# Gated linear attention and a four-expert MLP on one core: D parts of the second layers last, attention steps of neighbouring blocks paired, state update in half-width matmuls

## Chip, cores, metric

One core of one Trainium2 chip. The metric is device time in microseconds (us) of the whole program, lower is better; medians of several executions, and ratios with a 95% interval.

## The reference

```python
# attention: B, H, S, D = 4, 8, 768, 48
for t in range(S):
    state = alpha[:, :, t, :, None] * state + einsum('bhd,bhe->bhde', k[:, :, t], v[:, :, t])
    y[:, :, t] = einsum('bhd,bhde->bhe', q[:, :, t], state)
x = y.transpose(0, 2, 1, 3).reshape(3072, 384)
# experts: 4 of them, 384 -> 1024 -> 384
p = probs / (probs.sum(-1, keepdims=True) + 1e-9)
for e in range(4):
    out += p[:, e:e+1] * (maximum(x @ w1[e], 0) @ w2[e])
```

## The kernel before

The 24 blocks of 128 rows ("units", six chunks of time for each of four batches) go through attention in order. They form seven groups, gi = 0 to 6, of 2, 4, 4, 4, 4, 4 and 2 blocks. While TensorE does the first and second layers of a group's four experts, the 17 steps of the next group's attention are strewn between its matmuls by a schedule that counts an estimated clock. From gi = 2 on both layers run on split fp32 values: an operand is kept as a top part, a low part, and a "D" part; a product is one sum over the top and low parts and a second sum with D.

The second layer of an expert, before: two blocks at a time, their main sums, then their D sums, in four PSUM banks (the memory that matmuls write their sums to) shared with the first layer. Half of each D part is made at once in the first layer, the rest during the second.

```python
kinds = [((0, 1), range(FCH - 2)), ((0, 1), range(FCH - 2, FCH)), ((2,), range(FCH))]
steps = [(part, i, fc) for parts, tiles in (kinds if halves_ else [((3,), range(FCH))])
         for part in parts for i in range(len(slots)) for fc in tiles]
for n, (part, i, fc) in enumerate(steps):
    ...
    if later and n % 4 == 3:
        make_dif(*later.popleft())                      # the D parts
    ...
    nc.tensor.matmul(sums[i][part // 2], lhsT=h[:, part], rhs=w, start=..., stop=...)
    if part >= 1 and fc == FCH - 1:
        # VectorE: acc += p * sum, frees the bank
        add_up(gi, e, slots[i], part // 2, sums[i][part // 2 if halves_ else 0])
```

The attention steps that matter here, by their number j: 7 first scores (sc, 64 instructions), 10 last copy of the queries by ScalarE (qb), 11 last scores (far and sc), 15 result (yps), 16 state update (sps). Tiles: dec0 to dec6 (products of decays), xT (the split input of the first layer), hT (hidden parts). The tiles of the pool that holds the stage's operands are laid out one after the other in SBUF: ..., dec0 to dec6 (products of decays; dec6 is 16 bytes a partition), xT (the split input of the first layer, its moving operand), x_raw, then the pool of hT (hidden parts) and acc.

Of the kernel before, what the change touches and what calls it, by code (L numbers as in the profile page):

```python
# [10 lines left out]
F32 = mybir.dt.float32  # L11
# [9 lines left out]
def kernel(  # L21
# [37 lines left out]
    nc = tc.nc  # L59

    B, H, S, D = q.shape
    E, DM, F = moe_w1.shape
    P = 128
    NCB = S // P
    NP = H // 2
# [78 lines left out]
    accs = {}  # L144


    BEATS = [*(0.055 * (j + 1) for j in range(11)), 0.69, 0.75, 0.8, 0.87, 0.94, 1.0]
    MARGIN = 6.0
    waiting = deque()
    clock = 0.0  # L150
# [1 line left out]


    split1 = lambda gi, e: gi > 0
    split2 = lambda gi, e: gi > 1
    makes = [lambda gi, e: gi == 0, lambda gi, e: gi == 1]


# [110 lines left out]
    def attention(u):  # L269
# [41 lines left out]
        def next_q(li):  # L311
            m = LEVELS[li]
            qv = halves(QT, m)[:, :, :, 1, :]
            dv = halved(decs[li])
            nc.vector.tensor_mul(qv, qv, spread(dv[:, :, :, 0], m))  # L315
            dec = work.tile([P, NP, P // (2 * m)], F32, name=f"dec{li}", bufs=1)
            nc.vector.tensor_mul(dec, dv[:, :, :, 0], dv[:, :, :, 1])
            decs.append(dec)

# [138 lines left out]

        if cb < NCB - 1:
            KB = AT  # L460
            sps = ps.tile([P, NP, 2, D], F32, name="sps", tag="w")
            for p in range(NP):
                nc.tensor.matmul(sps[:, p], lhsT=KB[:, p, :], rhs=rv[:, 2 * p:2 * p + 2, :D],  # L463
                                 start=True, stop=True)
            for i in range(2):
                rows = slice(HD * i, HD * (i + 1))
                old, add = st[rows, :, i, :], sps[rows, :, i, :]
                if cb == 0:
                    nc.vector.tensor_copy(out=old, in_=add)
                else:  # L470
                    nc.vector.tensor_mul(old, old, decs[-1][rows].broadcast_to([HD, NP, D]))
                    nc.vector.tensor_add(old, old, add)
# [30 lines left out]
    def up(gi, e, fc, slots=None):  # L503
# [26 lines left out]
        if not split1(gi, e):  # L530
            for kc in range(KC):
                nc.tensor.matmul(one, lhsT=w[:, kc], rhs=xraws[gi][:, kc, lo:hi],  # L532
                                 start=(kc == 0), stop=(kc == KC - 1))
            nc.scalar.activation(out=whole, in_=one, func=ACT.Relu)
        else:
            two = ps.tile([P, NT], F32, name="two", tag="g", bufs=4)[:, :n]
            for out, terms in ((one, (1, 0)), (two, (2,))):
                for part in terms:
                    for kc in range(KC):
                        nc.tensor.matmul(out, lhsT=w[:, part, kc], rhs=x_part(gi, part, kc),  # L540
                                         start=(part == terms[0] and kc == 0),
                                         stop=(part == terms[-1] and kc == KC - 1))

            ends_first = gi < LAST
            for steps in finish:
                for _ in steps if ends_first else [next(steps)]:
                    pass
            ahead = [] if ends_first else list(finish)
            finish.clear()
            t = work.tile([P, NT], F32, name="t")[:, :n]  # L550
            nc.scalar.activation(out=t, in_=one, func=ACT.Copy, scale=FINE)  # L551
            if split2(gi, e):
                nc.vector.tensor_add(t, t, two)  # L553
                for steps in ahead:
                    next(steps, None)
                finish.append(hidden_parts(t, parts))
            else:
                nc.vector.tensor_add(whole, t, two)  # L558
                finish.append(rectified(whole))
# [16 lines left out]
    def hidden_parts(x, parts):  # L576
        top, low, dif = parts
        nc.scalar.activation(out=top, in_=x, func=ACT.Relu, scale=TRIM)  # L578
        yield
        nc.vector.scalar_tensor_tensor(out=low, in0=x, scalar=0.0, in1=top.bitcast(F32),  # L580
                                       op0=ALU.max, op1=ALU.subtract)

        n = x.shape[-1]
        at = n // 2 if n == NT else 0
        if at:
            make_dif(*(part[:, :at] for part in parts))
        later.append([part[:, at:] for part in parts])

    def make_dif(top, low, dif):
        nc.vector.scalar_tensor_tensor(out=dif, in0=top.bitcast(F32), scalar=1 / 4096.0,  # L590
# [6 lines left out]
    def down(gi, e, slots, between):  # L597


        first = first_piece(gi, e)  # L600
        halves_ = split2(gi, e)
        if slots[0] == 0 and makes[1](gi, e):
            making.extend(split_piece(1, first + k) for k in range(NQ))
        if slots[0] == 0 and makes[0](gi, e) and 0 < e < E - 1:
            making.extend(split_piece(0, first + k) for k in range(2, NQ))
        sums = [[ps.tile([P, DM], F32, name=f"ops{j}", tag="g", bufs=4)
                 for j in range(2 if halves_ else 1)] for _ in slots]

        kinds = [((0, 1), range(FCH - 2)), ((0, 1), range(FCH - 2, FCH)), ((2,), range(FCH))]
        steps = [(part, i, fc) for parts, tiles in (kinds if halves_ else [((3,), range(FCH))])  # L610
                 for part in parts for i in range(len(slots)) for fc in tiles]
        for n, (part, i, fc) in enumerate(steps):
            c, f = divmod(fc, FPQ)
            h = hidden[c][:, :, f, slots[i] * P:(slots[i] + 1) * P]
            advance(cost(1, gi, e) / FCH / (3 if halves_ else 1))
            while between and n >= between[0][0] * len(steps):
                between.popleft()[1]()
            if n == len(steps) // 2:
                background()
            if later and n % 4 == 3:  # L620
                make_dif(*later.popleft())
            if halves_:
                w = wt[1][first + c].rearrange("p t (c d) -> p t c d", d=DM)[:, part, f]
                nc.tensor.matmul(sums[i][part // 2], lhsT=h[:, part], rhs=w,  # L624
                                 start=(fc == 0 and part != 1), stop=(fc == FCH - 1 and part != 0))
            else:
                w = wt[1][first + c].rearrange("p (c d) -> p c d", d=DM)[:, f]
                nc.tensor.matmul(sums[i][0], lhsT=h[:, 2].bitcast(F32), rhs=w,  # L628
                                 start=(fc == 0), stop=(fc == FCH - 1))
            if part >= 1 and fc == FCH - 1:  # L630
                add_up(gi, e, slots[i], part // 2, sums[i][part // 2 if halves_ else 0])
        while between:
            between.popleft()[1]()
        background()
        if slots[-1] == len(groups[gi]) - 1 and gi != LAST - 1:
            while makes[1](gi, e) and (making or splitting):
                background()

            for c in range(NQ):
                del wt[1][first + c]  # L640
                if c < NQ // 2 or gi == LAST:
                    load_piece(1, first + NQ + c)
                else:
                    late.append(first + NQ + c)
# [31 lines left out]
    def deal():  # L676
# [3 lines left out]
        wanted = [0.0]  # L680
        ends = [0.0, 0.0]
        events = []
        t = 0.0
        for (gi, e), after in zip(tasks, tasks[1:]):
            part = 1 - 1 / len(groups[0]) if gi == e == 0 else 1
# [5 lines left out]
        for gis in [*([gi] for gi in range(1, LAST - 1)), [LAST - 1, LAST]]:  # L691
            gi, due = gis[0], wanted[gis[-1]] - MARGIN
            n = sum(len(groups[i]) for i in gis)
            first = wanted[gi - 1] if gi > 1 else 0.0
            space = (due - first) / (n if gi > 1 else (n + 1) / 2)
            if gi == 1:
                space /= 2
            for k in range(n):
                u = sum(map(len, groups[:gi])) + k
                end = due - (n - 1 - k) * space  # L700
                begin = max(end - 2 * space, ends[-2])
                ends.append(end)
                run = attention(u)
                events += [(begin + (end - begin) * beat, u, run) for beat in BEATS]
        return sorted(events, key=lambda x: x[:2])

    def advance(spent):
# [5 lines left out]
    with tc.manual_schedule():  # L713
# [48 lines left out]
        for (gi, e), after in zip(tasks, [*tasks[1:], (None, None)]):  # L762
            rest = gi == e == 0
            for fc in range(FCH):
                up(gi, e, fc, slice(1, len(groups[0])) if rest else None)
                advance(cost(0, gi, e) / (2 if rest else 1))
            each = 2 if split2(gi, e) else 1
            turns = [range(k, k + each) for k in range(rest, len(groups[gi]), each)]
            for k, slots in enumerate(turns):

                between = deque()
                if after[1] == 0:
                    for step, at in enumerate((0.0, 0.52, 0.62, 0.72)):
                        at = at * len(turns) - k
                        if 0 <= at < 1:
                            between.append((at, lambda step=step: split_x(after[0], step)))
# [31 lines left out]
```

## Time and profile before

| | before |
|---|---|
| time, median (lowest to highest) | 1073.79 us (1073.01 to 1075.13), 3 runs |
| span of the profiled run | 1071.6 us |
| busy: TensorE, weight loads, VectorE, ScalarE | 98%, 84%, 72%, 53% |
| DMA | 235 GB/s mean |

Busy time adds up the durations of instructions; TensorE's matmuls overlap (the 512-column ones last 400 ns in the profile, and the next starts 229 ns after), so its busy share says that it is never idle for long, not how fast it runs. For that, take the distance from start to start in the timeline. The lines on which the argument rests are in the prediction below.

### The profile page before, as it was taken

What the parts mean: (1) busy time and instruction counts of PE and PEld (TensorE: products, weight loads), DVE (VectorE), ACT (ScalarE), POOL (GpSimd) and SP (SyncE); (2) the same over time, 40 slices, a digit from 0 to 9 for tenths busy, and PEclk for the clock granted to TensorE, in tenths of its full rate; (3) what the DMA queues carried; (4) which work ended last, traced back from release to release, by engine and by line L of the source; (5) the groups of instructions that cost most, each with busy time, mean ns of one, the idle gap of its engine ahead of it and who ended that gap; (6) DMA issues with size and microseconds to landing.
All of it is one profiled execution on the core that took longest, in us unless ns stands there. A gap on an engine that the chain in (4) does not pass through costs nothing.

```text
span 1071.6 us, 21614 instructions
## 1 busy us (share of the span) xinstructions
PE 1048.1 (98%) x8460; PEld 899.1 (84%) x8460; DVE 775.2 (72%) x1711; ACT 566.7 (53%) x1202; POOL 32.7 (3%) x71
## 2 busy tenths in 40 slices
PE   8899999999999999999999999999999999999998
PEld 8777777676776798898898898898889889898988
DVE  5488776656566978778877777986787866666565
ACT  5687866575656554536546445555464543323232
POOL 2010000000000100000000000000000000000000
PEclk9999999999999999999999999999999999999999
DMA  8597699687696967758759558586594543544540
GB/s 123 156 330 216 230 328 368 238 328 241 236 309 209 402 216 274 281 160 312 268 170 359 204 187 337 186 281 234 158 358 173 221 192 147 207 177 178 187 181 31
DMA packets 158838, 251.67 MB, mean 235 GB/s; under 512 B 120112, under 2 KB 135344, under 8 KB 136208
## 3 DMA queue, kind: packets, MB, share of 16 engines
q1 hardware_dynamic: 149600, 208.82, 57.1%
q0 software_dynamic: 5760, 41.29, 9.8%
q8 instruction: 67, 1.10, 0.4%
q10 hardware_dynamic: 3376, 0.17, 0.3%
q14 instruction: 35, 0.29, 0.1%
HBM read 207.79 MB, written 42.47 MB: 234 GB/s over the span
## 4 chain that ended last, share of the span: by engine, by line
PE 83%; DVE 8%; ACT 6%; issue 2%; DMA 1%; SPq 0%; DVEq 0%; ACTq 0%
PE ops L624 25%; PE one L540 21%; PE ops L628 10%; PE two L540 10%; PE sc L334 6%; PE yps L428 3%; PE tp L266 3%; PE one L532 2%; ACT qb L308 2%; PE far L389 1%; PE sps L463 1%; DVE near L344 1%; DVE t L553 1%; DVE hT L580 1%; DVE hT L590 1%
## 5 line engine op out<-in xcount | busy, mean ns | idle before, releaser
L624 PE MATMUL ops<-w,hT 128*128 128x384 f32 x1728 | 318.0, 339 | 4.4 <-DVE acc L658 4.3
L624 PEld LDWEIGHTS ops<-w,hT 128*128 128x128 f32 x1728 | 299.1, 188 | 9.9 <-DVE acc L658 5.6
L540 PE MATMUL one<-xT,w 128*128 128x512 f32 x960 | 253.8, 400 | 2.6 <-DVE xT L248 1.1
L540 PEld LDWEIGHTS one<-xT,w 128*128 128x128 f32 x960 | 176.3, 188 | 41.8 <-DVE QT L315 1.6
L551 ACT ACTIVATE t<-one 128x512 f32<-128x512 f32 (+1 forms) x192 | 106.3, 554 | 153.6 <-PE one L540 148.5
L308 ACT COPY qb<-QT 64x256 f32<-64x256 f32 x336 | 136.4, 406 | 77.0 <-DVE QT L289 44.1
L578 ACT ACTIVATE hT<-t 128x512 fp32r<-128x512 f32 (+1 forms) x160 | 94.3, 589 | 123.6 <-DVE t L553 122.9
L580 DVE SCALAR_TENSOR_TENSOR hT<-t,hT 128x512 fp32r<-128x512 f32 (+1 forms) x160 | 102.2, 638 | 55.7 <-ACT hT L578 53.6
L540 PE MATMUL two<-xT,w 128*128 128x512 f32 x480 | 136.7, 393 | 0.0
L628 PE MATMUL ops<-hT 128*128 128x384 f32 x384 | 133.4, 491 | 0.0
L553 DVE TENSOR_TENSOR t<-t,two 128x512 f32<-128x512 f32 (+1 forms) x160 | 100.8, 630 | 41.9 <-ACT t L551 21.4
L590 DVE SCALAR_TENSOR_TENSOR hT<-hT 128x256 fp32r<-128x256 f32 x288 | 111.9, 422 | 4.4
L540 PEld LDWEIGHTS two<-xT,w 128*128 128x128 f32 x480 | 90.6, 189 | 20.0
L628 PEld LDWEIGHTS ops<-hT 128*128 128x128 f32 x384 | 69.5, 190 | 40.1 <-issue 0.4
L315 DVE TENSOR_TENSOR QT<-QT,dec 128x256 f32<-128x256 f32 x144 | 60.8, 422 | 38.2 <-ACT qb L308 37.5
L344 DVE COPY_PREDICATED near<-masks,sc 128x256 f32<-128x256 uint8 x144 | 77.0, 535 | 15.5 <-PE sc L334 12.8
L334 PEld LDWEIGHTS sc<-qb,KT 128*64 128x64 f32 x2304 | 72.7, 138 | 9.7 <-issue 5.6
L334 PE MATMUL sc<-qb,KT 128*64 128x64 f32 x2304 | 77.2, 223 | 2.6 <-ACT qb L308 2.6
L658 DVE SCALAR_TENSOR_TENSOR acc<-ops,p_all,acc 128x384 f32<-128x384 f32 x82 | 49.5, 614 | 33.9 <-PE ops L624 14.5
L326 ACT COPY KT<-KT 128x256 f32<-128x256 f32 x144 | 59.9, 416 | 3.2
L327 DVE TENSOR_TENSOR KT<-KT,dec 128x256 f32<-128x256 f32 x144 | 60.3, 419 | 0.0
L558 DVE TENSOR_TENSOR hT<-t,two 128x512 f32<-128x512 f32 x32 | 22.0, 688 | 35.6 <-ACT t L551 23.0
(88 smaller groups left out, 970.7 us busy)
## 6 DMA issues: line engine op xcount, KB each, us to landing
w<-kept SPq DMA_DIRECT2D x144, 1152.0 KB
kept<-w POOLq DMA_DIRECT2D x32, 1152.0 KB, 7.4
hT<-in_moe_w_dram SPq DMA_DIRECT2D x32, 384.0 KB
w<-in_moe_w_dram SPq DMA_DIRECT2D x48, 128.0 KB
ra<-in_alpha_dram SPq DMA_DIRECT2D x23, 192.0 KB
rk<-in_k_dram SPq DMA_DIRECT2D x23, 192.0 KB
rq<-in_q_dram SPq DMA_DIRECT2D x23, 192.0 KB
out_dram<-acc POOLq DMA_DIRECT2D x18, 192.0 KB, 6.6
```

What stands on the lines that cost most here:

```text
L308: nc.scalar.copy(out=qb[rows, :, i, :].rearrange("p a (b r) -> p a b r", r=m), in_=qv[rows])
L315: nc.vector.tensor_mul(qv, qv, spread(dv[:, :, :, 0], m))
L334: nc.tensor.matmul(out[HALF * s:HALF * (s + 1), 2 * p:2 * p + 2, :], lhsT=KTs[li][:, p, HALF * s:HALF * (s + 1)], rhs=qbs[li][:, p, :, QUA ...
L344: nc.vector.copy_predicated(near.rearrange("p a (b two r) -> p a b two r", two=2, r=m)[:, :, :, 1, :], mk.unsqueeze(1).broadcast_to([P, H, ...
L540: nc.tensor.matmul(out, lhsT=w[:, part, kc], rhs=x_part(gi, part, kc), start=(part == terms[0] and kc == 0), stop=(part == terms[-1] and k ...
L551: nc.scalar.activation(out=t, in_=one, func=ACT.Copy, scale=FINE)
L553: nc.vector.tensor_add(t, t, two)
L578: nc.scalar.activation(out=top, in_=x, func=ACT.Relu, scale=TRIM)
L580: nc.vector.scalar_tensor_tensor(out=low, in0=x, scalar=0.0, in1=top.bitcast(F32), op0=ALU.max, op1=ALU.subtract)
L590: nc.vector.scalar_tensor_tensor(out=dif, in0=top.bitcast(F32), scalar=1 / 4096.0, in1=low.bitcast(F32), op0=ALU.mult, op1=ALU.subtract)
L624: nc.tensor.matmul(sums[i][part // 2], lhsT=h[:, part], rhs=w, start=(fc == 0 and part != 1), stop=(fc == FCH - 1 and part != 0))
L628: nc.tensor.matmul(sums[i][0], lhsT=h[:, 2].bitcast(F32), rhs=w, start=(fc == 0), stop=(fc == FCH - 1))
```

## The change

Intent: no second layer waits for VectorE to free a bank between its two pairs of blocks; VectorE makes each D part in one instruction of 512 columns instead of two of 256; attention's small matmuls in the 64-column mode stand together, so that TensorE changes its mode less often; and the state update, of which only two quarters are needed, computes those two alone, side by side.

```diff
+    IN_PAIRS = [*(0.0425 * (j + 1) for j in range(8)), 0.385, 0.43, 0.475, 0.52, 0.6, 0.67, 0.755, 0.84, 1.02]
+    TOGETHER = ((15, 7), (16, 11))          # step of a unit, step of the next one
+    pairs_from = half + 2 * B
 ...
-            dec = work.tile([P, NP, P // (2 * m)], F32, name=f"dec{li}", bufs=1)
+            dec = work.tile([P, NP, P // (2 * m)], F32, name=f"dec{li}", bufs=1 + (li == 6))
 ...
-                nc.tensor.matmul(sps[:, p], lhsT=KB[:, p, :], rhs=rv[:, 2 * p:2 * p + 2, :D],
-                                 start=True, stop=True)
+                for i in range(2) if apart_ else [slice(0, 2)]:
+                    rows = slice(HD * i, HD * (i + 1)) if apart_ else slice(0, P)
+                    nc.tensor.matmul(
+                        sps[rows, p], lhsT=KB[:, p, rows],
+                        rhs=rv[:, 2 * p + i, :D] if apart_ else rv[:, 2 * p:2 * p + 2, :D],
+                        start=True, stop=True)
 ...                                          # hidden_parts: D parts only later
-        at = n // 2 if n == NT else 0
-        if at:
-            make_dif(*(part[:, :at] for part in parts))
-        later.append([part[:, at:] for part in parts])
+        later.append(parts)
 ...                                          # down: the second layer
-        kinds = [((0, 1), range(FCH - 2)), ((0, 1), range(FCH - 2, FCH)), ((2,), range(FCH))]
+        pairs = [slots[k:k + 2] for k in range(0, len(slots), 2)]
+        sides = [[((0, 1), in_parts[:-2]), ((0, 1), in_parts[-2:])], [((3,), whole), ((2,), in_parts)]]
+        steps = [(side, slot, part, fc) for side in range(2) for pair in pairs
+                 for parts, tiles in sides[side] for part in parts for slot in pair for fc in tiles]
 ...
-            if later and n % 4 == 3:
+            if later and n % (len(steps) // 12 - 1) == len(steps) // 12 - 2:
                 make_dif(*later.popleft())
 ...                                          # deal: the schedule
-            first = wanted[gi - 1] if gi > 1 else 0.0
+            first = wanted[gi - 1] - MARGIN * (2 < gi < LAST - 1) if gi > 1 else 0.0
 ...
+                due_at = {-1: begin, **{j: begin + (end - begin) * beats[j + 1] for j in (7, 11, 16)}}
+                for ahead, j in TOGETHER if pairs else ():
+                    if (u > pairs_from or j == 11) and abs(times[-1][ahead] - due_at[j]) < space / 6:
+                        due_at[j] = times[-1][ahead]
 ...                                          # the other steps between those; the loop over slots
-            each = 2 if split2(gi, e) else 1
+            each = len(groups[gi]) if split2(gi, e) else 1
 ...                                          # the splits of x for the next group, later
-                    for step, at in enumerate((0.0, 0.52, 0.62, 0.72)):
+                    for step, at in enumerate((0.0, 0.6, 0.7, 0.78)):
```

The second buffer of dec6 is needed because the next unit now makes its dec6 (step 10) before this unit's state update (step 16) has read its own.

More of the change, by code (lines that the diff above doesn't have):

```diff
@@ L154 @@
     split1 = lambda gi, e: gi > 0
-    split2 = lambda gi, e: gi > 1
+    split2 = lambda gi, e, c=0: gi > 1
     makes = [lambda gi, e: gi == 0, lambda gi, e: gi == 1]
@@ L460, in attention @@
             KB = AT
-            sps = ps.tile([P, NP, 2, D], F32, name="sps", tag="w")
+            apart_ = u + 1 >= pairs_from
+            sps = ps.tile([P, NP, 1 if apart_ else 2, D], F32, name="sps", tag="w")
             for p in range(NP):
-                nc.tensor.matmul(sps[:, p], lhsT=KB[:, p, :], rhs=rv[:, 2 * p:2 * p + 2, :D],
-                                 start=True, stop=True)
+                for i in range(2) if apart_ else [slice(0, 2)]:
[4 more added lines that the diff above has]
+                        start=True, stop=True)
             for i in range(2):
                 rows = slice(HD * i, HD * (i + 1))
-                old, add = st[rows, :, i, :], sps[rows, :, i, :]
+                old, add = st[rows, :, i, :], sps[rows, :, 0 if apart_ else i, :]
                 if cb == 0:
@@ L551, in up @@
             nc.scalar.activation(out=t, in_=one, func=ACT.Copy, scale=FINE)
-            if split2(gi, e):
+            if split2(gi, e, c):
                 nc.vector.tensor_add(t, t, two)
@@ L581, in hidden_parts @@
                                        op0=ALU.max, op1=ALU.subtract)
-        n = x.shape[-1]
-        at = n // 2 if n == NT else 0
-        if at:
-            make_dif(*(part[:, :at] for part in parts))
-        later.append([part[:, at:] for part in parts])
+        later.append(parts)
     def make_dif(top, low, dif):
@@ L600, in down @@
         first = first_piece(gi, e)
-        halves_ = split2(gi, e)
+        in_parts = [fc for fc in range(FCH) if split2(gi, e, fc // FPQ)]
+        whole = [fc for fc in range(FCH) if fc not in in_parts]
         if slots[0] == 0 and makes[1](gi, e):
-            making.extend(split_piece(1, first + k) for k in range(NQ))
+            making.extend(split_piece(1, first + k) for k in range(NQ) if not split2(gi, e, k))
         if slots[0] == 0 and makes[0](gi, e) and 0 < e < E - 1:
             making.extend(split_piece(0, first + k) for k in range(2, NQ))
-        sums = [[ps.tile([P, DM], F32, name=f"ops{j}", tag="g", bufs=4)
-                 for j in range(2 if halves_ else 1)] for _ in slots]
@@ L609, in down @@
-        kinds = [((0, 1), range(FCH - 2)), ((0, 1), range(FCH - 2, FCH)), ((2,), range(FCH))]
-        steps = [(part, i, fc) for parts, tiles in (kinds if halves_ else [((3,), range(FCH))])
-                 for part in parts for i in range(len(slots)) for fc in tiles]
-        for n, (part, i, fc) in enumerate(steps):
+        pairs = [slots[k:k + 2] for k in range(0, len(slots), 2)]
+        sides = [[((0, 1), in_parts[:-2]), ((0, 1), in_parts[-2:])], [((3,), whole), ((2,), in_parts)]]
+        steps = [(side, slot, part, fc) for side in range(2) for pair in pairs
+                 for parts, tiles in sides[side] for part in parts for slot in pair for fc in tiles]
@@ L613, in down @@
+        begins = {key: n for n, key in reversed([*enumerate(step[:2] for step in steps)])}
+        ends = {step[:2]: n for n, step in enumerate(steps)}
+        sums = {}
+        for n, (side, slot, part, fc) in enumerate(steps):
             c, f = divmod(fc, FPQ)
-            h = hidden[c][:, :, f, slots[i] * P:(slots[i] + 1) * P]
-            advance(cost(1, gi, e) / FCH / (3 if halves_ else 1))
+            advance(cost(1, gi, e) * len(slots) / len(steps))
             while between and n >= between[0][0] * len(steps):
@@ L617, in down @@
                 between.popleft()[1]()
-            if n == len(steps) // 2:
+            if n and n % (len(steps) // (2 * len(slots))) == 0:
                 background()
-            if later and n % 4 == 3:
+            if later and n % (len(steps) // 12 - 1) == len(steps) // 12 - 2:
                 make_dif(*later.popleft())
-            if halves_:
+            at = (side, slot)
+            if n == begins[at]:
+                sums[at] = ps.tile([P, DM], F32, name="ops", tag="g", bufs=4)
@@ L623, in down @@
+            h = hidden[c][:, :, f, slot * P:(slot + 1) * P]
+            if part < 3:
                 w = wt[1][first + c].rearrange("p t (c d) -> p t c d", d=DM)[:, part, f]
-                nc.tensor.matmul(sums[i][part // 2], lhsT=h[:, part], rhs=w,
-                                 start=(fc == 0 and part != 1), stop=(fc == FCH - 1 and part != 0))
+                h = h[:, part]
             else:
                 w = wt[1][first + c].rearrange("p (c d) -> p c d", d=DM)[:, f]
-                nc.tensor.matmul(sums[i][0], lhsT=h[:, 2].bitcast(F32), rhs=w,
-                                 start=(fc == 0), stop=(fc == FCH - 1))
@@ L630, in down @@
-            if part >= 1 and fc == FCH - 1:
-                add_up(gi, e, slots[i], part // 2, sums[i][part // 2 if halves_ else 0])
+                h = h[:, 2].bitcast(F32)
+            nc.tensor.matmul(sums[at], lhsT=h, rhs=w, start=(n == begins[at]), stop=(n == ends[at]))
+            if n == ends[at]:
+                add_up(gi, e, slot, side, sums.pop(at))
         while between:
@@ L682, in deal @@
         events = []
+        times = []
         t = 0.0
@@ L703, in deal @@
                 run = attention(u)
-                events += [(begin + (end - begin) * beat, u, run) for beat in BEATS]
+                pairs = u >= pairs_from
+                beats = [0.0, *(IN_PAIRS if pairs else BEATS)]
+                due_at = {-1: begin, **{j: begin + (end - begin) * beats[j + 1] for j in (7, 11, 16)}}
+                for ahead, j in TOGETHER if pairs else ():
+                    if (u > pairs_from or j == 11) and abs(times[-1][ahead] - due_at[j]) < space / 6:
+                        due_at[j] = times[-1][ahead]
+                marks = sorted(due_at)
+                times.append([])
+                for lo, hi in zip(marks, marks[1:]):
+                    times[-1] += [due_at[hi] if j == hi else
+                                  due_at[lo] + (due_at[hi] - due_at[lo]) * (beats[j + 1] - beats[lo + 1])
+                                  / (beats[hi + 1] - beats[lo + 1]) for j in range(lo + 1, hi + 1)]
+                for j, ahead in ((6, 13), (12, 15)):
+                    if times[:-1]:
+                        times[-1][j] = max(times[-1][j], times[-2][ahead] + 0.5)
+                events += [(time, u, run) for time in times[-1]]
         return sorted(events, key=lambda x: x[:2])
```

## The prediction

> **What bounds the kernel now.** I read the page first: busy shares, slices, the chain that ended last, the costliest groups.
>
> ```profile
> PE 1048.1 (98%) x8460; PEld 899.1 (84%) x8460; DVE 775.2 (72%) x1711; ACT 566.7 (53%) x1202; POOL 32.7 (3%) x71
> PE   8899999999999999999999999999999999999998
> PE 83%; DVE 8%; ACT 6%; issue 2%; DMA 1%; SPq 0%; DVEq 0%; ACTq 0%
> L624 PE MATMUL ops<-w,hT 128*128 128x384 f32 x1728 | 318.0, 339 | 4.4 <-DVE acc L658 4.3
> L624 PEld LDWEIGHTS ops<-w,hT 128*128 128x128 f32 x1728 | 299.1, 188 | 9.9 <-DVE acc L658 5.6
> L590 DVE SCALAR_TENSOR_TENSOR hT<-hT 128x256 fp32r<-128x256 f32 x288 | 111.9, 422 | 4.4
> ```
>
> TensorE is the bound from end to end. It is short of work only in the first slices and for a few microseconds later; those later gaps of the second layer (L624) are put down almost wholly to one thing, the VectorE addition into acc (L658) that frees a PSUM bank. A gain can therefore come from two places only: less TensorE time, or fewer of these gaps. VectorE at 72% has room on average, so making its work shorter is not itself a gain.
>
> Busy time of pipelined matmuls says little about their cost, so next I read TensorE's timeline in a steady stage (440 to 520 us) and took start to start. Columns: start, duration of the group, engine, line, tiles, count.
>
> ```profile
> 450.56 1.53 PE L540 MATMUL one<-xT,w 128*128 128x512 f32 x6
> 451.93 0.85 PE L540 MATMUL two<-xT,w 128*128 128x512 f32 x3
> 452.62 1.02 PE L463 MATMUL sps<-rv,AT 128*128 128x96 f32 x8
> 453.42 1.63 PE L540 MATMUL one<-xT,w 128*128 128x512 f32 x6
> 454.90 0.85 PE L540 MATMUL two<-xT,w 128*128 128x512 f32 x3
> ...
> 495.65 2.08 PE L334 MATMUL sc<-qb,KT 128*64 128x64 f32 x64
> 497.67 1.65 PE L540 MATMUL one<-xT,w 128*128 128x512 f32 x6
> 499.16 0.85 PE L540 MATMUL two<-xT,w 128*128 128x512 f32 x3
> ```
>
> Six undisturbed first-layer matmuls take 451.93 - 450.56 = 1.37 us, 229 ns each. The state update (sps, 8 instructions) takes 453.42 - 452.62 = 0.80 us and the six after it 1.48 us, 0.11 more: 0.91 us in all. The first scores, alone, take 2.02 us for 64 instructions, 31.6 ns each because two 64-column halves run at once, and the six after them 1.49 us: 0.12 us for going back. Three matmuls started at 494.88 should have ended at 495.57, so the burst began 0.08 late: about 0.20 us to enter and leave the 64-column mode. In other rows of this view the second layer runs at 174 ns a matmul.
>
> Last I looked for the gaps. In the 756 to 768 us stretch:
>
> ```profile
> 755.68 7.58 PE L624 MATMUL ops<-w,hT 128*128 128x384 f32 x42
> ...
> 760.37 0.76 DVE L590 SCALAR_TENSOR_TENSOR hT<-hT 128x256 fp32r<-128x256 f32 x2
> ...
> 761.92 1.43 DVE L590 SCALAR_TENSOR_TENSOR hT<-hT 128x256 fp32r<-128x256 f32 x4
> ...
> 764.16 0.42 DVE L590 SCALAR_TENSOR_TENSOR hT<-hT 128x256 fp32r<-128x256 f32 x1
> 764.50 0.61 DVE L658 SCALAR_TENSOR_TENSOR acc<-ops,p_fine,acc 128x384 f32<-128x384 f32 x1
> ...
> 765.17 2.35 PE L624 MATMUL ops<-w,hT 128*128 128x384 f32 x12 [1.90 <-DVE acc L658]
> ```
>
> The first pair of blocks is done, the second pair wants its bank back, and the addition that frees it stands in VectorE's queue behind the D parts (L590) and behind attention work. TensorE stands for about 2 us. The same happens near 592, 676 and 850 us, for 0.6 to 1.6 us, and shorter near 458.
>
> **What the Trainium skill says.** "TensorEngine Tiling (Array Packing)", section Key Properties: "Changing tiling mode (not just tile) drains the TensorE". The trace agrees: the 0.20 us above. The same page, same section, has different tiles load and multiply in parallel; the trace agrees with 31.6 ns per score instruction against 100 ns (0.80 / 8) per full-width update. "PSUM — Partial Sum Buffer", Specifications: eight banks per partition. This kernel's pools take 4 + 2 + 2 one-bank buffers, so nothing is spare and the order of sums decides who waits. "TensorE: Matmul & The Clock Gate", Architectural detail, calls VectorE and ScalarE strict FIFO; the stretch above shows it, the urgent addition last in a row of ready D parts.
>
> **The change, part by part.**
>
> *State update in 64-column halves, behind it the last scores of the next unit.* It replaces 8 instructions of full width (128 weights columns, 96 moving) by 16 of half width (64 and 48), two at a time. It applies to units 9 to 19, 11 of them. By the score row I put 16 x about 30 ns = 0.48 us (estimate; fewer moving columns, same weights). If it stands directly ahead of far and sc, which run in the same mode, it adds no switch: 0.91 - 0.48 = 0.43 us gained. By the schedule's own arithmetic, step 16 at 1.02 of a unit's two spaces coincides with step 11 at 0.52 of the next, which begins one space later; the two are forced equal if closer than a sixth of a space. At the border to the last two groups the space drops from 33.2 to 26.7 (clock units of the schedule), the two lie some 5.7 apart against a limit of 4.5, and that one stays alone: 0.91 - 0.68 = 0.23. Sum 10 x 0.43 + 0.23 = **4.5 us**.
>
> *First scores behind the result.* Both are already together in most units before (0.94 against 0.44 and half a unit): the timeline has yps and sc as one burst for all but two of the border cases it touches (yps at 486.69 with sc at 495.65, and 653.97 with 662.94). Joining saves one enter-and-leave, 0.20 us. The shifted start of each group (MARGIN) closes the first; the second keeps its distance by the arithmetic above. **0.2 us**.
>
> *Second layers with D last.* Matmuls are the same 96 for each expert of a four-block group. What moves: both pairs' main sums come first in four different banks, the D sums of all four after step 64. The second pair no longer waits for the first pair's addition, and the first bank is wanted again only at step 64, 33 matmuls or 5.7 us after its sum ended near step 30. That should remove the waits on acc: 5.6 us on the load row (4.3 on the matmul row, whose modelled ends cover part of each gap). I take **5.6 us**.
> VectorE: today 288 D instructions of 256 columns, 288 x 422 ns = 122 us; afterwards 128 of 512 at about the 638 ns of the equally shaped L580 and 32 of 256, 95 us. It is about 26 us less VectorE work, none of it on the path by itself. Its first-layer load falls from 0.630 + 0.638 + 0.422 = 1.69 us per 2.06 us step to 1.27, and the work goes to the second layer.
>
> *Other parts.* The twin buffer for the last decay and the later x splits add no work. No DMA changes in size. Sum: 4.5 + 0.2 + 5.6 = 10.3 us, which alone would give 1063.5.
>
> **The rivals.** (1) *The D products become the new wait.* The eight D parts are issued at steps 6 to 55 and the first product that reads them is step 64: nine matmuls, 1.6 us. The stretch above shows VectorE 2 to 3 us behind in its queue. For it: FIFO and less slack than before, when half the D parts were made in the first layer. Against: the first layer leaves VectorE 0.42 us a step lighter, so it enters the second with less of a backlog. Twelve second layers have attention beside them; 12 x 1.5 us would give 18 us back, 1082. I expect two or three short ones, 1 us. (2) *Scores wait for ScalarE.* Between the last query copy and the last scores the schedule now leaves 0.045 x 66.4 = 3.0 instead of 0.085 x 63.4 = 5.4 clock units, and the early levels come closer together. The trace knows this chain:
>
> ```profile
> DVE QT L315 <- ACT qb L308: 45.7, 42, 7.5
> ```
>
> 42 waits, mostly harmless to TensorE today; once, near 714 us, the far products waited 0.2 us for such a copy. Fourteen units at 0.5 us would make 7 us, 1070; I expect 1 us. (3) *More than the sum*: the chain has 14% on VectorE and ScalarE, and if lighter first layers shortened that, the time could fall under 1055. Against it: at 229 and 174 ns start to start TensorE is nearly never late outside the gaps counted, so that share of the chain is mostly parallel to it. (4) *Nothing*: bank waits move to the end of the D sums; 1069.
>
> **Time, range and chances.** 1063.5 + 1 + 1 = 1065.5 us, 0.8% less. Below, all gains whole plus some small gaps closed, 1058; above, rivals 1 and 2 together eating most, 1072. Faster by over 2% needs 1052, twice the sum: 3%. Slower by over 2% needs 1095, rival 1 at more than its worst: 2%.
>
> **What would show it.** sps as 16 instructions of 64 columns, about 0.5 us, directly ahead of far in ten units; yps and sc together for unit 14; the L624 rows without their wait on acc; D instructions 160 in number and some 90 to 95 us. Wrong would be: a wait of L624 on hT (D parts), of far or sc on the query copies worth over 3 us, or a slower matmul rate.

## The result and the profile after

1070.51 us (1069.11 to 1071.44, 4 runs) against 1074.46 us for the kernel before in the same comparison (4 runs): ratio 0.9964, interval 0.9946 to 0.9981. Ratios are the mean time of one kernel's fast runs over that of the other's in the same rounds, so not quite the ratio of the medians. The change gains 0.4%, about 3.9 us, and 8.3 were forecast. The time is inside the stated range, near its slow end, and more than half of the forecast gain is missing, so the working has a hole.

The page of the kernel after, the lines that answer to those of before:

```profile
PE 1043.6 (98%) x8548; PEld 892.0 (84%) x8548; DVE 759.8 (71%) x1583; ACT 570.3 (53%) x1202; POOL 32.8 (3%) x71
PE 86%; ACT 5%; DVE 5%; DMA 2%; issue 2%; SPq 0%; ACTq 0%; DVEq 0%
L641 PE MATMUL ops<-w,hT 128*128 128x384 f32 x1728 | 314.0, 339 | 0.0
L641 PEld LDWEIGHTS ops<-w,hT 128*128 128x128 f32 x1728 | 299.1, 188 | 2.2 <-ACT t L561 0.6
L596 DVE SCALAR_TENSOR_TENSOR hT<-hT 128x512 fp32r<-128x512 f32 (+1 forms) x160 | 92.7, 632 | 0.0
```

The second layer's waits on acc are gone (4.4 us of idle before, 0.0 now), the D instructions are 160 and 92.7 us, inside the forecast 90 to 95. (The row counts overlapping time once. Counted as the prediction did, number times mean, they are 101 us; see the part on why it was wrong.) The state update and its neighbours, from the timeline of TensorE:

```profile
451.62 0.86 PE L550 MATMUL two<-xT,w 128*128 128x512 f32 x3
452.41 0.67 PE L471 MATMUL sps<-rv,AT 128*64 128x48 f32 x16
452.91 0.62 PE L394 MATMUL far<-qb,KT 128*64 128x128 f32 x8
453.36 1.10 PE L339 MATMUL sc<-qb,KT 128*64 128x64 f32 x32
454.39 1.67 PE L550 MATMUL one<-xT,w 128*128 128x512 f32 x6
```

452.91 - 452.41 = 0.50 us for the update, directly ahead of far, as forecast (0.48). The 16 small matmuls start in pairs 6 to 7 ns apart, a pair every 58 ns: two halves run at once. So the gains are there. What is new stands in two other places. The first is the group of the far products, before (3.1 us of idle) and after:

```profile
L389 PE MATMUL far<-qb,KT 128*64 128x128 f32 x192 | 15.8, 285 | 3.1 <-ACT qb L308 3.1
L394 PE MATMUL far<-qb,KT 128*64 128x128 f32 x192 | 15.4, 282 | 6.8 <-ACT qb L313 4.2 <-DVE hT L590 2.7
```

The second can be seen only start to start. Three rows of the tail, where no attention is left and both kernels run the same first layer, before:

```profile
914.62 1.54 PE L540 MATMUL one<-xT,w 128*128 128x512 f32 x6
916.00 0.85 PE L540 MATMUL two<-xT,w 128*128 128x512 f32 x3
916.68 1.53 PE L540 MATMUL one<-xT,w 128*128 128x512 f32 x6
```

and after:

```profile
909.60 1.57 PE L550 MATMUL one<-xT,w 128*128 128x512 f32 x6
911.00 0.86 PE L550 MATMUL two<-xT,w 128*128 128x512 f32 x3
911.70 1.56 PE L550 MATMUL one<-xT,w 128*128 128x512 f32 x6
```

Nine matmuls take 2.06 us before and 2.10 after. The unmerged starts show how regular this is: in the tail the distances repeat every three matmuls, 226, 229, 232 ns before and 231, 232, 237 ns after.

To see where all the time went I summed the distances from start to start of all matmuls, from the first second-layer matmul of gi = 1 on (187.6 us before, 186.5 after), and split them; the table is called the ledger below. "Plain" is 229, 174, 120 and 323 ns for the four kinds of large matmul, the same 731.0 us for all kernels, and left out; "rate" is what undisturbed large matmuls take beyond it; "attention" is everything of the small matmuls with entering and leaving; "far" and "other" are TensorE's waits, over about 0.13 us each.

| us | first-layer rate | second-layer rate | attention | far waits | other waits | sum with 731.0 |
|---|---|---|---|---|---|---|
| before | 0.5 | -0.2 | 140.8 | 0.2 | 7.5 | 879.8 |
| after | 5.5 | -0.9 | 135.1 | 4.0 | 1.9 | 876.6 |
| difference | +5.0 | -0.6 | -5.7 | +3.8 | -5.6 | -3.2 |

The remaining 1.1 us lie ahead of the mark. They seem to belong to the new second layers, in a way that nothing forecast: the mark stands at 187.6 to 187.8 us in the four kernels with the old second layers, at 185.7 to 187.4 in the ten with the new. The sums and the waits in the ledger hardly depend on where "undisturbed" begins, but another cut moves 2 to 3 us between the attention column and the second-layer rate, so differences of these two are sure to about 1.5 us only. Forecast were -4.7 for attention, -5.6 for the waits on the additions and +2 for rivals. The two gains came in, 11.3 us instead of 10.3. Against them stand 3.8 us of waits for the far products and 5.0 us of a slower first layer, whose code and order in the tail did not change.

### The profile page after: what moved, and what is told of

Its sections match the earlier page's. It is cut to its first block, busy times and chain, and to the rows that moved or that the text cites. A ratio compares the mean times of both kernels' runs of the same rounds, so it can differ in the third digit from the quotient of the medians.

```text
span 1067.3 us, 21698 instructions
## 1 busy us (share of the span) xinstructions
PE 1043.6 (98%) x8548; PEld 892.0 (84%) x8548; DVE 759.8 (71%) x1583; ACT 570.3 (53%) x1202; POOL 32.8 (3%) x71
## 4 chain that ended last, share of the span: by engine, by line
PE 86%; ACT 5%; DVE 5%; DMA 2%; issue 2%; SPq 0%; ACTq 0%; DVEq 0%
PE ops L641 36%; PE one L550 22%; PE two L550 11%; PE sc L339 6%; PE yps L433 3%; PE tp L271 3%; PE one L542 2%; ACT qb L313 2%; PE far L394 1%; DMA w<-kept 1%; PE sps L471 1%; DVE near L349 1%; DMA kept<-w 1%; DVE w L233 1%; DMA rq<-in_q_dram 1%
## 5 line engine op out<-in xcount | busy, mean ns | idle before, releaser
L641 PE MATMUL ops<-w,hT 128*128 128x384 f32 x1728 | 314.0, 339 | 0.0
L588 ACT ACTIVATE hT<-t 128x512 fp32r<-128x512 f32 (+1 forms) x160 | 94.2, 589 | 81.9 <-DVE t L563 81.9
L563 DVE TENSOR_TENSOR t<-t,two 128x512 f32<-128x512 f32 (+1 forms) x160 | 101.2, 632 | 49.9 <-PE two L550 29.9
L596 DVE SCALAR_TENSOR_TENSOR hT<-hT 128x512 fp32r<-128x512 f32 (+1 forms) x160 | 92.7, 632 | 0.0
L542 PE MATMUL one<-xT,w 128*128 128x256 f32 (+1 forms) x240 | 46.0, 340 | 0.6 <-ACT xT L449 0.6
```

Of the source, the lines that this page charges most:

```text
L542: nc.tensor.matmul(one, lhsT=w[:, kc], rhs=xraws[gi][:, kc, lo:hi], start=(kc == 0), stop=(kc == KC - 1))
L563: nc.vector.tensor_add(t, t, two)
L588: nc.scalar.activation(out=top, in_=x, func=ACT.Relu, scale=TRIM)
L596: nc.vector.scalar_tensor_tensor(out=dif, in0=top.bitcast(F32), scalar=1 / 4096.0, in1=low.bitcast(F32), op0=ALU.mult, op1=ALU.subtract)
L641: nc.tensor.matmul(sums[at], lhsT=h, rhs=w, start=(n == begins[at]), stop=(n == ends[at]))
```

## The experiments

The theory after this reading: (T1) the slower first layer comes from the second buffer of dec6, which moves xT, x_raw, hT and acc by 32 bytes a partition (the allocator rounds 16 up); (T2) the far waits belong to two units whose last scores fall right behind the end of a first layer. The rivals: the rate belongs to the new order of instructions or to what VectorE does beside the first layer; the waits belong to the squeezed steps in general. Addresses below are byte offsets in a partition, as the built programs have them; xT is at 147424 before and at 147456 after. Rates are means of undisturbed first-layer distances after 380 us.

### Twin buffer alone

```diff
 # kernel before
-            dec = ..., name=f"dec{li}", bufs=1)
+            dec = ..., name=f"dec{li}", bufs=1 + (li == 6))
```

> The kernel before with the second buffer of the last decay alone: 16 more bytes of data per partition, which the allocator rounds to 32, so that xT, the hidden parts and the accumulators start 32 bytes later (a multiple of 64 instead of 32 over one). Placement theory: the first-layer matmuls of 512 columns go from a mean of 229 ns start to start to about 233, as in the changed kernel, 1440 x 4.3 ns = 6 us, so about 5 to 6 us slower than before. Rival (the slower rate comes from what VectorE and ScalarE do beside the first layer, or from the new order): no difference, within 1 us, rate 229.

Measured: 1075.94 us against 1073.25, ratio 1.0018 (1.0004 to 1.0033). The rate is 233.4 ns, in the rhythm 231, 232, 237 of the kernel after, from a kernel that differs from before in nothing but addresses. The rate term of the ledger rose by 5.0 us as expected, but the time by less: the second layer's rate gained 0.9 us and the waits on the additions fell by 1.1 us, perhaps because a slower first layer leaves VectorE more time; that is not shown. So T1's cause is shown for the rate, and the rival falls, but the forecast of 5 to 6 us for the time was a miss: 1.9 us by the ratio.

### The kernel after, xT moved on to 147488

```diff
 # kernel after
-name=f"dec{li}", bufs=1 + (li == 6))
+name=f"dec{li}", bufs=1 + 2 * (li == 6))
```

> The changed kernel with three buffers instead of two for the last decay, so that xT lies 64 bytes after its place in the kernel before: same place within 64 bytes. Placement theory: rate back to 229 ns, 5 to 6 us faster than the changed kernel, about 1065. Rival: same as the changed kernel, rate 233.

A miss: 1071.72 us, ratio 0.9981 (0.9968 to 0.9994). The rate is 232.7 ns in a third rhythm that repeats every seven matmuls, and the second layer is slower too (175.9 against 174.2 ns). Being at the same place within 64 bytes does not bring the rate back. My rule was wrong, the placement theory as such still open.

### D last alone

The second-layer hunks of the change on the kernel before, addresses as before.

```diff
 # kernel before
+ hidden_parts, down and the loop over slots as after; dec, sps, IN_PAIRS and deal as before
```

> Only the second layers with D last; addresses as before. If the sum of the prediction holds for this term: no wait of the second layer on the additions, no wait on D parts, 5 us faster than before (1069). Rival 1 of the prediction: new waits of the second layer on the D parts take 2 us or more of that back.

1067.57 us, ratio 0.9943 (0.9930 to 0.9956): 6.1 us gained, more than the whole change. Its groups of the second layer:

```profile
L631 PE MATMUL ops<-w,hT 128*128 128x384 f32 x1728 | 316.4, 339 | 0.0
L631 PEld LDWEIGHTS ops<-w,hT 128*128 128x128 f32 x1728 | 300.5, 188 | 2.5 <-ACT t L551 0.6
```

No wait on acc and none on the D parts: the prediction's term holds, and its first rival does not occur. In its ledger the other waits fell by 4.7 us, and 1.5 us more are gained ahead of the mark.

### Paired steps alone

```diff
 # kernel before
+ IN_PAIRS, TOGETHER, half-width sps and deal as after
+ dec6 with bufs=3 (xT at 147488); hidden_parts and down as before
```

> Only the pairing of attention steps with the half-width state update, second layers as before, three decay buffers so that xT keeps its place within 64 bytes. By the ledger of starts: ten joined bursts 0.43 us shorter each, one joined result, 4.5 us gained, less the waits of the far products for the query copies at the borders of groups, 2.6 and 1.2 us in the changed kernel if they come here too: 1 to 5 us faster than before. If the waits on the additions grow with the new times of attention work, less.

A miss by far: 1084.92 us, ratio 1.0107 (1.0092 to 1.0122), 11.5 us slower. In its ledger: rates +6.2 us (4.0 first, 2.2 second layer), far waits +7.1, other waits +1.0, attention only -3.1. I had counted on the loss of rate ending at 147488, which the run beside it disproved, and on no more far waits than in the kernel after.

### The kernel after with all tiles in the place of before

The second dec6 goes behind all other tiles; the stream of instructions is that of the kernel after.

```diff
 # kernel after
+    last = ctx.enter_context(tc.tile_pool(name="last", bufs=1))     # opened after hid
-            dec = work.tile(..., name=f"dec{li}", bufs=1 + (li == 6))
+            dec = (last if li == 6 and u % 2 else work).tile(..., name=f"dec{li}", bufs=1)
```

> The changed kernel, instruction for instruction, but the second buffer of the last decay lies behind all other tiles, so xT, the hidden parts and the accumulators have the addresses of the kernel before. Placement theory: first-layer starts again in the rhythm 226, 229, 232 ns (mean about 229.5 to 230.1 as in the kernel before and in the D-last one) instead of 231, 232, 237 (233.4), second layer 174 to 175; 1440 x 3.5 ns = 5 us faster than the changed kernel, about 1065.5. Rival (the rhythm belongs to the changed instruction order and the 64-byte move failed for that reason): 233.4 stays, 1070.5.

1064.65 us, ratio 0.9923 (0.9910 to 0.9937); the kernel after, run again beside it, has 0.9980. That is 0.57%, 6.1 us, for another place of a 16-byte buffer. The tail's timeline:

```profile
908.59 1.54 PE L551 MATMUL one<-xT,w 128*128 128x512 f32 x6
909.97 0.85 PE L551 MATMUL two<-xT,w 128*128 128x512 f32 x3
910.65 1.54 PE L551 MATMUL one<-xT,w 128*128 128x512 f32 x6
```

Nine matmuls take 2.06 us again, the rhythm is 226, 229, 232 and the rate 229.3 ns. Placement it is, not the order of instructions.

### The two far waits

In the kernel after, the first of the two waits, rows of TensorE and ScalarE:

```profile
663.85 1.20 PE L641 MATMUL ops<-w,hT 128*128 128x384 f32 x6
664.35 0.63 ACT L588 ACTIVATE hT<-t 128x512 fp32r<-128x512 f32 x1 [1.30 <-DVE t L563]
...
666.33 0.63 ACT L588 ACTIVATE hT<-t 128x512 fp32r<-128x512 f32 x1 [0.87 <-DVE t L563]
666.87 0.80 ACT L313 COPY qb<-QT 64x256 f32<-64x256 f32 x2
...
667.72 0.66 PE L394 MATMUL far<-qb,KT 128*64 128x128 f32 x8 [2.66 <-DVE hT L590]
```

The first layer has ended six matmuls earlier. ScalarE and VectorE are still passing its last hidden parts to each other (L588 waits for L563, which waits for ScalarE again), and the query copy that far needs stands behind them in ScalarE's queue. The wait was put down to "DVE hT", but what had to end was the copy at 666.87. The same happens near 838 us. These are units 18 and 23; the edit delays their last scores, and with them in proportion the steps between the marks 7, 11 and 16 of the schedule.

```diff
 # kernel after
                         due_at[j] = times[-1][ahead]
+                if u in (18, 23):
+                    due_at[11] += 4.0
```

> The changed kernel with the last scores of two units (18 and 23), which stood a few matmuls after the end of a first layer, 4 clock units later. Theory: the waits of 2.6 and 1.2 us of the far products on the query copies go away, since these copies only stand behind the finish of the first layer in the ScalarE and VectorE queues: 3.5 us faster than the changed kernel, 1067. Rival: the waits move with the step, or the later step makes a wait of its own (near the result or the border of the next group): under 1 us gained.

1066.76 us, ratio 0.9946 (0.9934 to 0.9959), against 0.9980 for the kernel after run beside it: 3.7 us. The ledger has far waits of 0.7 instead of 4.0 us, at an unchanged rate of 233.4 ns. Unit 18's scores in this kernel:

```profile
669.08 0.42 PE L641 MATMUL ops<-w,hT 128*128 128x384 f32 x1
670.01 0.66 PE L394 MATMUL far<-qb,KT 128*64 128x128 f32 x8 [0.51 <-ACT qb L313]
```

Of its wait 0.5 us are left.

### Both corrections

```diff
 # e5_same_place
+                if u in (18, 23):
+                    due_at[11] += 4.0
```

> Both corrections together. If they are independent, 5 + 3.5 us off the changed kernel: about 1062, which would be 5 us under the D-last part alone (1067.6), the 5 to 6 us of the shorter attention bursts. If the pairing of steps is worth nothing beyond the two corrections, 1067.

1062.17 us, ratio 0.9901 (0.9886 to 0.9916). The two corrections add up within the noise (8.5 us together, 6.1 and 3.7 alone), and this version beats before and after. Against D last alone it gains another 0.4%; here, at last, the shorter bursts of attention pay.

### The kernel after again

> The changed kernel unchanged, for a second profile. If the rhythm of the first layer belongs to the program, 231, 232, 237 ns again and the mean within 0.3 ns of 233.4; if it is drawn anew in each execution, another rhythm or a mixture, and then no placement theory can be read from single profiles.

1070.50 us, ratio 0.9980 (0.9966 to 0.9993); 231, 232, 237 ns once more, mean 233.4. Two executions of the program, in different comparisons, have the same rhythm.

### Which tile's place

```diff
 # e9: e5 with hT and acc alone 32 bytes on
+    hid.tile([P, 8], F32, name="gap", bufs=1)
 # e10: kernel after (xT at 147456), hT and acc 2048 bytes from their place in before
+    hid.tile([P, 504], F32, name="gap", bufs=1)
```

> As e5 (all tiles in the place of the kernel before), then the hidden parts and accumulators alone 32 bytes on, where the changed kernel has them. If the place of xT, which the first layer streams, makes the rhythm: mean 229 to 230 ns, time as e5, 1064.7. If the place of the hidden parts does: 233.4 ns and 1070.

> The changed kernel with xT and x_raw where it has them, the hidden parts and accumulators 2048 bytes from their place in the kernel before. If the place of xT makes the rhythm: 231, 232, 237 ns, mean 233.4, time as the changed kernel, 1070.5. If the place of the hidden parts does: 229.5 ns and about 1065.

e9: 1064.34 us, ratio 0.9926 (0.9906 to 0.9947), first-layer rate 229.1. e10: 1071.66 us, ratio 0.9989 (0.9974 to 1.0005), rate 233.4. The first layer's rate follows xT (with x_raw behind it), not hT. The second layer, which loads hT as weights, seems to follow hT a little: 175.5 ns in e10 against 174.2 in the kernel after, where hT alone differs, but only 173.4 in e9 against 174.0 in e5. It is 175.9 in e2 and e4, and 173.6 to 175.0 in the others; the kernels with every tile in the place of before span 174.0 to 175.0 by themselves, so this is not settled.

### Pairing alone, without its two losses

```diff
 # e4 with the second dec6 in the pool "last" (all tiles as before), and units 18 and 23 later as in e6
```

> The paired attention steps alone, all tiles in the place of the kernel before, and the last scores of units 18 and 23 later: e4 without its two known losses. e4 lost 11.5 us; of that 6.2 was rate and 5.2 the two waits of the far products at 672 and 852 us. So 1073, about as before: the 6 us of shorter bursts are then eaten by longer waits on the additions that only the D-last part removes. If the pairing pays on its own, 1067.

1074.63 us, ratio 1.0014 (0.9993 to 1.0035): as before, within noise. The second layer's row:

```profile
L635 PE MATMUL ops<-w,hT 128*128 128x384 f32 x1728 | 319.2, 340 | 7.1 <-DVE acc L669 5.4 <-DVE t L564 1.7
```

Its waits are longer than in the kernel before (4.4): other waits are 11.7 us in the ledger, +4.2, and far waits 2.5, +2.3, which eat the attention term of -3.2. That paired steps bring VectorE their work in larger lumps would explain it; no run tests that. The two halves of the change are not independent: pairing alone gains nothing that can be measured, and on top of D last, with both corrections, it gains 0.4%.

### A fourth place

```diff
 # e7 with both dec6 buffers in the pool "last": xT at 147392
```

> The best kernel so far (e7) with xT, hidden parts and accumulators 32 bytes earlier than in the kernel before, a fourth place. No theory says which rhythm this gives; if place matters and not the mere fact of a move from 32 to 0 over a multiple of 64, the mean may differ from both 229.5 and 233.4 ns. 229.5 would leave 1062, 233.4 would make 1067.5.

1065.79 us, ratio 0.9938 (0.9921 to 0.9955), rate 233.2 ns in a fourth rhythm. With the same stream of instructions as e7 it is 3.6 us slower by the medians, 4.0 by the ratios (the two were timed in different comparisons). All places together:

| xT at | first-layer rate, ns | in |
|---|---|---|
| 147392 | 233.2 | e12 |
| 147424 | 229.1 to 230.1 | before, e3, e5, e7, e9, e11 |
| 147456 | 233.4 | after, e1, e6, e8, e10 |
| 147488 | 232.6, 232.7 | e2, e4 |

## Why the prediction was wrong

- **The state update and the pairs** (4.5 + 0.2): right. Ten updates joined and one alone, as worked out from the schedule; each joined burst costs 0.47 us more than far and sc alone, where 0.48 stood. The one alone costs 0.81 us, not 0.68. The attention term gave 5.7 us; read burst by burst the named items come to about 4.7, and the other 1 us was not traced. One reading behind it was wrong without harm: the 0.12 us "for going back" is not the price of the mode. The first six large matmuls after the full-width update, where no mode changes, are late by 0.10 us too; only the 0.09 us on entering goes with the narrow modes (the full-width updates begin on time, within 0.01 us).
- **D last** (5.6): right. Other waits fell by 5.6 us, and D last alone gained 6.1 us; that this is so close has some luck in it, as 4.7 us of waits and 1.5 us ahead of the mark make it up. The side sum on VectorE's work was off: 638 ns is a mean over two widths. The 512-column D instruction takes 685 ns, so the D work fell by 20 us (122 to 101), not 26; and by the same mixed means the first layer's load on VectorE is nearer 1.80 us than 1.69 of each 2.06. No wait came of it.
- **First rival, waits on D parts** (1 us allowed): did not occur; no second-layer row has such a wait.
- **Second rival, scores waiting for ScalarE** (1 us allowed): right in kind, wrong in size and place. It cost 3.8 us, not spread over fourteen units but in two, at the end of a first layer. I took the narrower distance between steps as the danger; the danger was a step falling where ScalarE and VectorE finish a layer in turns. Delaying two steps gave 3.7 us back.
- **"The twin buffer for the last decay and the later x splits add no work"**: this is the step that failed. The buffer adds no work, and I stopped there; it moves xT, and the first layer ran 5.0 us slower. "A slower matmul rate" stood in the list of what would make the prediction wrong, but with no term in the sum. With all tiles in the old place the same stream of instructions takes 1064.65 us; the forecast was 1065.5. So the forecast was close to a kernel without that move, but by luck: rival 2 was 2.8 us too small, the gains were 1 us too small, and the 1 us allowed for rival 1 was not spent.

Open is why a place gives a rhythm. The distances repeat every three, four (e12) or seven (e2) matmuls, while the weights come from four changing buffers, so it looks like matmuls, weight loads and reads of the moving operand settling into a common step; no run here shows what of it an address shifts. Nor is place all: in the tail of e3 two first layers of the four ran at 233, 233, 234 ns, e7 has one such layer, and one in e5 averaged 231.9, all with xT at 147424. A whole layer of 72 matmuls at that rate costs about 0.3 us more. Each rate comes from a single profiled execution of its kernel (the kernel after has two). Whether a better place than 147424 exists was not searched.

## What to carry to other kernels

A new buffer, however small, moves every tile allocated behind it; when a kernel is bound by TensorE to 98%, compare the start-to-start distance of its commonest matmul before and after each change, and put small additions behind the large operands. Steps that need a ScalarE or VectorE result should not be placed just behind the end of a layer, where these two engines hand its last tiles back and forth (here 3.7 us for two steps). A gain that depends on slack elsewhere (here the pairs on D last) should be tried in the order in which it needs the slack, since alone it can show nothing.

## What the Trainium skill lacked or had wrong

- "SBUF — State Buffer", Operand start alignment, says of itself that it is "about legality, not speed", and no page has what the place of a moving operand costs: four places of xT, 32 bytes apart and all legal, gave 229.1 to 230.1, 232.7, 233.2 and 233.4 ns for a 512-column matmul, up to 6.1 us of this kernel.
- "TensorE: Matmul & The Clock Gate", Part 1 (Wait — 56ns, not 53.3ns?), gives 215.7 ns start to start for 512 columns of bf16 with a warm clock. The fp32r stream here, with a weight load for each matmul, never had it as a mean: 229 to 233 ns at a granted clock of 0.995 to 1.0, in repeating rhythms that no page mentions.
- "TensorEngine Tiling (Array Packing)", Key Properties, says that a change of tiling mode drains TensorE, but not what that costs: here 0.09 to 0.10 us on entering a narrow mode from full-width matmuls. The 0.10 to 0.13 us after leaving it can't be put down to the mode, as full-width groups of small matmuls leave 0.08 to 0.12 us behind them too.
